# A convolution kernel before and after: the inverse transform over b in three tiles of 120 rows, one channel of its sums moved by DMA, and the stages issued as finer steps in another order

## The chip, the core and the metric

The kernel runs on one core of a Trainium2 chip. A core has five engines that run side by side and meet only at semaphores: TensorE (PE, matrix products; its weight loads are shown as PEld), VectorE (DVE), ScalarE (ACT), GpSimd (POOL) and SyncE (SP, which here only issues DMAs). Each works through its own instructions in order. The metric is the device time of one execution in microseconds.

## What is computed

The reference is a long convolution followed by two layers of experts, cut here to its lines of arithmetic:

```python
h_filt = (np.maximum(pos_emb @ w1, 0.0) @ w2) * np.exp(-0.01 * pos)[:, None]
u = x * v                                    # (2, 12480, 128)
y = np.fft.irfft(np.fft.rfft(u, n=2*S, axis=1) * np.fft.rfft(h_filt, n=2*S, axis=0)[None], n=2*S, axis=1)[:, :S, :]
x = (x * y).reshape(B * S, D)
h = x @ moe_w_in                             # 128 -> 2048
x = np.where(h > 0, h, np.exp(np.minimum(h, 0)) - 1) @ moe_w_out
h = x @ moe2_w_in
return (h * np.cos(h)) @ moe2_w_out
```

The kernel computes the convolution with a transform of its own. A sequence is laid out as NA = 98 rows (a) of NB = 128 (b), and the transform is taken over a (NF = 90 frequencies, real and imaginary part), twiddled, taken over b, multiplied by the transform of the filter, and taken back over b and then over a.

## The kernel before

The program has three stages. First the filter's taps are computed (to about 47 us). Then comes the convolution, to about 690 us: 32 chunks (NCH) of DC = 4 channels, each with three passes k: the two batches (k = 0, 1) and the filter (k = 2). The last stage runs the two expert layers (from about 694 us to the end). Beside the convolution the experts' weights are decoded in 32 jobs (`top` and `low`: small steps on ACT, DVE and GpSimd, and stores to `w_d`).

One pass of a chunk goes through these steps; the line numbers are those of the profile:

- `prod`: u = x * v on GpSimd (L321).
- `st_a`: four fp32 products over a into `ps_a` (L340, 180 columns each), two DVE products with the twiddles (za, zb, L345), one GpSimd sum (z, L348). For k = 2 ACT copies z to fp32r (zh, L97), and `lo_z` takes the rest (zl, L359) on GpSimd.
- `st_b`: the transform over b into `ps_b` (L376, 360 columns): four fp32 products for the batches, twelve fp32r products (high and low parts) for the filter. For the filter ACT copies the sums out (hr, hi, L381 to L383). For the batches DVE multiplies them by the filter's transform (L389, L390) and adds (y, L392); ACT copies y to fp32r (yh, L97), and `lo_y` takes the rest (yl, L332) on GpSimd.
- `st_c`: the inverse transform over b (L408). For each of the four channels the stationary operand is y's slice of 90 columns and the moving operand 256 columns of the table: six products for each channel, into its quarter of `ps_c` (90 partitions x 1024). Then two DVE products with the table ti (wa, wb, L412) and one GpSimd sum (w, L419; for the last chunk half of it on DVE, L417).
- `st_d`: the inverse transform over a (L426): two fp32 products of 512 columns, contracted over w's 90 partitions, into `ps_d`; DVE multiplies by x (at, L428), and SP stores it to `xt_d`, from where the experts' stage reads it.

An fp32 product is issued as two instructions in the trace. `ps_a`, `ps_b` and `ps_c` each have one pair of PSUM banks and `ps_d` one bank, so a product into such a buffer waits until the readers of its last contents are done. Where the last chunk's `ps_c` of k = 1 is concerned, it takes the pair of `ps_a`.

The order is written out by hand: within `tc.manual_schedule()` each engine issues in the order in which the program calls the steps. The tuple `steps` is the body of one period; an entry (f, back, k) runs step f for the chunk of `back` periods ago. So a chunk's passes are spread over three periods, and `st_c` and `st_d` of k = 1 run two periods after `st_a`. At the end of each period `load(p + 2)` issues the DMAs for x and v of a later chunk on SP. When the last period is through, ACT issues the loads of the first expert layer's weights and of its first x tile, which waits for the store of the last chunk's k = 0.

## Time and profile before

| | us |
|---|---|
| device time, median of 3 executions (lowest, highest) | 2923.79 (2923.07, 2927.09) |
| span of the profiled execution | 2922.3 |
| PE busy | 2888.7 (99%) |
| PEld busy | 2393.3 (82%) |
| DVE busy | 2497.0 (85%) |
| ACT busy | 2146.6 (73%) |
| POOL busy | 2632.8 (90%) |

The span counts from the first to the last instruction of the profiled execution; its own device time is not listed apart, and the median stands 1.5 us above the span. The busy shares are means over stages that differ: in the convolution ACT is busy for three tenths, among the experts for nearly nine. The granted TensorE clock, as a mean over the execution, is 0.995 of full speed; it is lower only at the start, at the run-in of the convolution (50 to 70 us) and between convolution and experts (690 to 710 us). A matmul's duration in the trace reaches into the next one, since they are pipelined; how long one takes of the engine's time is read from start to start.

### The profile page before, as it was taken

Reading aid. Unit: us, or ns where it says so; the run is one execution under the profiler, and the core shown is the slowest. Engines: PE = TensorE matmul, PEld = TensorE weight load, DVE = VectorE, ACT = ScalarE, POOL = GpSimd, SP = SyncE. Lnnn points to the kernel's source line nnn. Section 1 sums busy time; section 2 is a strip of 40 time slices with the busy share of each in tenths; the row PEclk is TensorE's granted clock in tenths of the full one; section 3 lists DMA queues with packets and bytes.
Section 4 is the critical chain, followed back from the end, with each engine's and each line's share of the span. In section 5 each row is a group of like instructions: output and inputs, shape, how many; then the busy total and the mean of one; then the engine's idle time right before and its main releaser. Section 6 shows DMA issues by size and latency. Waiting matters only on the chain.

```text
span 2922.3 us, 40341 instructions
## 1 busy us (share of the span) xinstructions
PE 2888.7 (99%) x13580; PEld 2393.3 (82%) x13580; DVE 2497.0 (85%) x3241; ACT 2146.6 (73%) x3332; POOL 2632.8 (90%) x1908
## 2 busy tenths in 40 slices
PE   8999999998999999999999999999999999999999
PEld 6878787886888888888888887888888888888887
DVE  5888888887998998899899998888888888888887
ACT  3322323224988898888888888888888888888887
POOL 4888888886999999999999998999999999999998
PEclk9999999998999999999999999999999999999999
DMA  3333333333000000000000001000000000000000
GB/s 105 90 81 88 97 89 86 88 83 97 14 11 14 11 12 14 14 11 11 14 11 14 11 11 60 11 14 11 14 11 14 11 11 14 11 14 11 13 12 14
DMA packets 83104, 96.82 MB, mean 33 GB/s; under 512 B 6106, under 2 KB 68088, under 8 KB 82898
## 3 DMA queue, kind: packets, MB, share of 16 engines
q1 hardware_dynamic: 77072, 88.20, 10.6%
q10 hardware_dynamic: 5826, 6.04, 0.7%
q8 instruction: 109, 1.79, 0.3%
q14 instruction: 97, 0.79, 0.1%
HBM read 59.94 MB, written 34.28 MB: 32 GB/s over the span
## 4 chain that ended last, share of the span: by engine, by line
PE 92%; ACT 3%; DVE 2%; issue 2%; POOL 1%; DMA 0%; ACTq 0%; POOLq 0%; DVEq 0%
PE h_ps L545 35%; PE o_ps L614 34%; PE ps_b L376 8%; PE ps_c L408 6%; PE ps_a L340 4%; PE ps_d L426 4%; ACT e L582 1%; DVE e L575 1%; DVE e L584 1%; ACT e L573 1%; PE h_ps L277 1%; ACT gh L97 1%; ACT ot L622 1%; PE w_ps L218 0%; PE r_ps L259 0%
## 5 line engine op out<-in xcount | busy, mean ns | idle before, releaser
L106 POOL TENSOR_TENSOR gl<-e,gh 128x960 fp32r<-128x960 f32 x780 | 1463.7, 1888 | 88.6 <-ACT gh L97 45.3
L545 PE MATMUL h_ps<-xh,w 128*128 128x480 f32 x3328 | 1022.3, 388 | 15.5 <-DVE e L562 5.5
L614 PE MATMUL o_ps<-gh,w 128*128 128x480 f32 x3120 | 933.0, 380 | 0.0
L545 PEld LDWEIGHTS h_ps<-xh,w 128*128 128x128 f32 x3328 | 623.0, 189 | 150.5 <-issue 26.6
L614 PEld LDWEIGHTS o_ps<-gh,w 128*128 128x128 f32 x3120 | 586.8, 188 | 92.9 <-POOL gh L105 0.2
L575 DVE SCALAR_TENSOR_TENSOR e<-e,h_ps 128x960 f32<-128x960 int32 x416 | 479.9, 1154 | 193.1 <-ACT e L573 67.0
L545 PE MATMUL h_ps<-xl,w 128*128 128x480 f32 x1664 | 634.6, 381 | 0.0
L560 DVE SCALAR_TENSOR_TENSOR e<-e,t_ps 128x480 f32<-128x480 f32 x832 | 539.6, 652 | 108.8 <-ACT t_ps L558 87.7
L614 PE MATMUL o_ps<-gl,w 128*128 128x480 f32 x1560 | 594.3, 381 | 2.0 <-POOL gl L106 2.0
L556 ACT ACTIVATE e<-h_ps 128x480 f32<-128x480 f32 x832 | 475.5, 572 | 141.6 <-PE h_ps L545 106.9
L573 ACT ACTIVATE e<-h_ps 128x960 int32<-128x960 f32 x416 | 404.1, 971 | 149.8 <-PE h_ps L545 148.0
L105 POOL TENSOR_SCALAR gh<-e 128x960 fp32r<-128x960 f32 x468 | 466.8, 998 | 42.1 <-DVE e L562 24.1
L558 ACT ACTIVATE t_ps<-h_ps 128x480 f32<-128x480 f32 x832 | 479.4, 576 | 0.0
L562 DVE SCALAR_TENSOR_TENSOR e<-e,h_ps 128x480 f32<-128x480 f32 x780 | 472.3, 647 | 0.0
L582 ACT ACTIVATE e<-e,half_pi 128x960 f32<-128x960 f32 x416 | 453.9, 1091 | 0.3 <-DVE e L575 0.3
L584 DVE TENSOR_TENSOR e<-e,h_ps 128x960 f32<-128x960 f32 x390 | 447.2, 1147 | 1.3 <-ACT e L582 1.2
L545 PEld LDWEIGHTS h_ps<-xl,w 128*128 128x128 f32 x1664 | 314.3, 189 | 52.3 <-POOL xl L106 0.6
L614 PEld LDWEIGHTS o_ps<-gl,w 128*128 128x128 f32 x1560 | 293.7, 188 | 50.6 <-POOL gl L106 3.2
L97 ACT ACTIVATE gh<-e 128x960 fp32r<-128x960 f32 x312 | 312.4, 1001 | 0.0
L376 PE MATMUL ps_b<-z_t,dft_t 128*128 128x360 f32 x512 | 165.7, 466 | 2.1 <-DVE y_t L392 1.7
L348 POOL TENSOR_TENSOR z_t<-za,zb 128x720 f32<-128x720 f32 x96 | 141.1, 1470 | 26.3 <-DVE zb L345 26.3
L408 PE MATMUL ps_c<-dft_h,yh 128*90 128x256 f32 x512 | 160.4, 313 | 0.0
(90 smaller groups left out, 3066.7 us busy)
## 6 DMA issues: line engine op xcount, KB each, us to landing
x_t<-in_x SPq DMA_DIRECT2D x32, 392.0 KB
v_t<-in_v SPq DMA_DIRECT2D x32, 392.0 KB
xt_d<-at SPq DMA_DIRECT2D x64, 196.0 KB
out<-ot SPq DMA_DIRECT2D x52, 240.0 KB
x_in<-xt_d SPq DMA_DIRECT2D x50, 240.0 KB
raw<-in_wi SPq DMA_DIRECT2D x16, 256.0 KB
w_d<-hi SPq DMA_DIRECT2D x32, 128.0 KB
w_d<-lo SPq DMA_DIRECT2D x32, 128.0 KB
```

The lines of the kernel that those rows point to most:

```text
L105: ENG[plan[0]].tensor_scalar(hi, full, 1.0, 0.0, op0=ALU.mult, op1=ALU.add)
L106: ENG[plan[1]].tensor_tensor(lo, full, hi.bitcast(F32), op=ALU.subtract)
L545: nc.tensor.matmul(h[:, 0:T], a, b, start=k == 0, stop=k == 2)
L556: nc.scalar.activation(u[:, e], hs[e][:, 0:T], AF.Exp)
L558: nc.scalar.activation(ts[e][:, 0:T], hs[e][:, 0:T], AF.Tanh, scale=0.5)
L560: nc.vector.scalar_tensor_tensor(u[:, e], u[:, e], 1.0, ts[e][:, 0:T], op0=ALU.add, op1=ALU.mult)
L562: nc.vector.scalar_tensor_tensor(gt[:, e], u[:, e], 0.0, hs[e][:, 0:T], op0=ALU.min, op1=ALU.max)
L573: nc.scalar.activation(kq, hv, AF.Copy, scale=1.0 / TWO_PI, bias=0.25)
L575: nc.vector.scalar_tensor_tensor(rr, kq, -TWO_PI, hv, op0=ALU.mult, op1=ALU.add)
L582: nc.scalar.activation(rr, rr, AF.Sin, bias=half_pi)
L584: nc.vector.tensor_tensor(gt, rr, hv, op=ALU.mult)
L614: nc.tensor.matmul(o, a, b[:, e], start=f == 0 and k == 0, stop=f == NFT - 1 and k == len(mm) - 1)
```

## The change

**Tiles of 120 rows.** y is written in another order: DVE's sum is split in two, so that the 4 x 90 columns of the four channels stand as three groups of 120: 90 columns of one of the first three channels and 30 of the fourth. The step `mm_c` takes each group as stationary operand: three tiles by six products, into 120 partitions x 768. The two products with ti and the sum w have that shape too. Rows 90 to 119 of w's three tiles are the fourth channel, in thirds; three DMAs on SP move them into a tile `v_w` of 90 partitions x 256. `mm_d` takes the first three channels from w (two products of 384 columns) and the fourth from `v_w` (two of 128). The table ti grows from 90 x 1024 to 120 x 1536 values.

**Filter products in another order.** In `mm_b` with k = 2 the eight products with zh come first and the four with zl last.

**Finer steps.** The stages are cut where they go from one engine to another: `mm_a` (A), `out_a` (a), `add_z` (z), `hi_z` (H), `lo_z` (L), `mm_b` (B), `out_h` (h), `mul_y` (y), `hi_y` (Y), `lo_y` (l), `mm_c` (C), `out_c` (c), `add_w` (w with its DMAs), `mm_d` (D), `out_d` (d), `prod` (u), `fetch` (x: the DMAs for x and v), `t` and `o` (the two halves of the decoding). One string gives the order: letter, periods back, pass. x and v are now fetched within the period, behind `d20`, for the chunk whose u is the period's last step. The last chunk's `ps_c` stays in its own pair of banks.

```diff
+NT = 3
+NM = DC * NF // NT
...
+    m = NM - NF
+    row = np.concatenate([np.repeat(np.arange(NF)[:, None], NT, 1),
+                          np.arange(m)[:, None] + m * np.arange(NT)[None, :]])[:, :, None]
+    ti = 2 * np.pi * ((2 * row + 1) * kr[None]) / (2 * L)
...
-            ti_t = const.tile([NF, 2, 4 * NB], F32, name="ti_t")
+            ti_t = const.tile([NM, 2, NT * 2 * NB], F32, name="ti_t")
...
+                def slot(n, name, at):
+                    return pa.tile([n, 2, 512], F32, name=name, tag=PS[at])
...
+                def mm_b(c, k, at):
...
+                        groups = (((dft_h, z[0]), (dft_l, z[0])), ((dft_h, z[1]),))
+                    for i, group in enumerate(groups):
+                        for r in range(2):
+                            mm = [(a[:, sl], b[:, q]) for sl, q in prs[r] for a, b in group]
+                            for j, (a, b) in enumerate(mm):
+                                nc.tensor.matmul(ps[:, r, 0:n], a, b, start=i == j == 0,
+                                                 stop=i == len(groups) - 1 and j == len(mm) - 1)
...
+                def mul_y(c, k, at):
...
-                    nc.vector.tensor_tensor(y, t1, pv[:, ::-1], op=ALU.add)
...
+                    q, m = pv[:, ::-1], NT * NF
+                    yv = y.rearrange("p r (i m) -> p r i m", i=NT)
+                    for o, a, b, e in ((slice(0, NF), 0, m, NT), (slice(NF, NM), m, n, NT)):
+                        nc.vector.tensor_tensor(yv[:, :, :, o], t1[:, :, a:b].rearrange("p r (i k) -> p r i k", i=e),
+                                                q[:, :, a:b].rearrange("p r (i k) -> p r i k", i=e), op=ALU.add)
+                    yy[c, k] = (y,)
+
+                def hi_y(c, k, at):
+                    yh = skewed(p2, [NB, 2, DC * NF], F32R, SKEW, name="yh")
+                    copy_r(yh, yy[c, k][0])
+                    yy[c, k] += (yh,)
...
+                def mm_c(c, k, at):
                     yh, yl = yy.pop((c, k))
-                    last = c == NCH - 1
-                    ps = pa.tile([NF, 2, 512], F32, name="ps_c", tag="ps_a" if last and k else "ps_c")
+                    ps = slot(NM, "ps_c", at or "c").rearrange("p a b -> p (a b)")
                     n = 2 * NB
-                    for s in range(DC):
-                        sl = slice(s * NF, (s + 1) * NF)
-                        o = ps[:, s // 2, (s % 2) * n:(s % 2 + 1) * n]
+                    for i in range(NT):
+                        sl = slice(i * NM, (i + 1) * NM)
                         mm = [(yt[:, r, sl], th[:, (1 - r) * NB:(3 - r) * NB])
                               for r in range(2) for yt, th in ((yh, dft_h), (yh, dft_l), (yl, dft_h))]
                         for j, (a, b) in enumerate(mm):
-                            nc.tensor.matmul(o, a, b, start=j == 0, stop=j == 5)
-                    t1 = p1.tile([NF, DC * n], F32, name="wa")
...
+                def out_c(c, k, at):
+                    ps, n = pcs.pop((c, k)), NT * 2 * NB
+                    t1 = p1.tile([NM, n], F32, name="wa")
+                    t2 = skewed(p1, [NM, n], F32, SKEW, name="wb")
                     for q, t in ((0, t1), (1, t2)):
-                        nc.vector.tensor_tensor(bank2(t), ps, ti_t[:, q:q + 1].to_broadcast([NF, 2, 512]), op=ALU.mult)
-                    w = p2.tile([NF, 2, DC, NB], F32, name="w_t")
-                    p, q = parts(t1, NB), parts(t2, NB)[:, ::-1]
-                    if last:
+                        nc.vector.tensor_tensor(t, ps[:, 0:n], ti_t[:, q], op=ALU.mult)
+                    wab[c, k] = t1, t2
+
+                def add_w(c, k, at):
+                    p, q = (t.rearrange("p (i r k) -> p i r k", i=NT, r=2) for t in wab.pop((c, k)))
+                    q = q[:, :, ::-1]
+                    w = p2.tile([NM, NT, 2, NB], F32, name="w_t")
+                    if c == NCH - 1:
                         nc.gpsimd.tensor_tensor(w[:, 0], p[:, 0], q[:, 0], op=ALU.add)
-                        nc.vector.tensor_tensor(w[:, 1], p[:, 1], q[:, 1], op=ALU.add)
+                        nc.vector.tensor_tensor(w[:, 1:NT], p[:, 1:NT], q[:, 1:NT], op=ALU.add)
                     else:
                         nc.gpsimd.tensor_tensor(w, p, q, op=ALU.add)
-                    ww[c, k] = w
-
-                def st_d(c, k):
-                    w = ww.pop((c, k))
-                    ps = pd.tile([NA, DC, NB], F32, name="ps_d")
-                    for r in range(2):
-                        nc.tensor.matmul(ps, g_t[:, r * NA:(r + 1) * NA], w[:, r], start=r == 0, stop=r == 1)
+                    v = p2.tile([NF, 2, NB], F32, name="v_w")
+                    m = NM - NF
+                    for i in range(NT):
+                        nc.sync.dma_start(v[i * m:(i + 1) * m], w[NF:NM, i])
+                    ww[c, k] = (w, v)
+
+                def mm_d(c, k, at):
+                    w, v = ww.pop((c, k))
+                    ps = pds[c, k] = pd.tile([NA, DC, NB], F32, name="ps_d")
+                    for o, rhs in ((ps[:, 0:NT], w[0:NF]), (ps[:, NT:DC], v.rearrange("p (i r) b -> p i r b", i=1))):
+                        for r in range(2):
+                            nc.tensor.matmul(o, g_t[:, r * NA:(r + 1) * NA], rhs[:, :, r], start=r == 0, stop=r == 1)
+
+                def out_d(c, k, at):
                     at = p2.tile([NA, DC, NB], F32, name="at")
-                    nc.vector.tensor_tensor(at, ps, xs[c][:, k], op=ALU.mult)
+                    nc.vector.tensor_tensor(at, pds.pop((c, k)), xs[c][:, k], op=ALU.mult)
...
-                steps = ((st_b, 1, 0), (prod, 0, 1), (top, 0, 0), (lo_y, 1, 0), (low, 0, 0), (top, 0, 1), (st_a, 0, 2),
-                         (st_c, 2, 1), (top, 0, 2), (lo_z, 0, 2), (low, 0, 1), (st_b, 1, 1), (st_a, 0, 0), (lo_y, 1, 1),
-                         (st_d, 2, 0), (low, 0, 2), (st_c, 1, 0), (prod, -1, 0), (st_b, 0, 2), (st_a, 0, 1), (top, 0, 3),
-                         (st_d, 2, 1))
-                for p in range(NCH + 2):
-                    for f, back, k in steps:
-                        if 0 <= p - back < NCH or f in (top, low):
-                            f(p - back, k)
-                    load(p + 2)
+                def fetch(c, k, at):
+                    if c not in xs:
+                        load(c)
+
+                FN = dict(u=prod, A=mm_a, a=out_a, z=add_z, H=hi_z, L=lo_z, B=mm_b, h=out_h, y=mul_y, Y=hi_y, l=lo_y,
+                          C=mm_c, c=out_c, w=add_w, D=mm_d, d=out_d, t=top, o=low, x=fetch)
+
+                def step(name, c, k, at=""):
+                    if name in "to" or 0 <= c < NCH:
+                        FN[name](c, k, at)
+
+                steps = """
+                    o t l10 a02 c21 B11 t y11 z02 H02 A00 D20 u01 C10 w21 a00 L02 d20 Y11 x-10 t
+                    z00 c10 B02 A01 a01 h02 l11 w10 z01 D21 o B00 t d21 y00 C11 A-12 Y00 o u-10
+""".split()
+                back = lambda s: (s[0], int(s[1:-1]) if len(s) > 1 else 0, int(s[-1]) if len(s) > 1 else 0)
+                for p in range(-2, NCH + 4):
+                    for f, b, k in map(back, steps):
+                        if f in "to" and not 0 <= p < NCH + 2:
+                            continue
+                        step(f, p - b, k)
```

How the order moves, at three places in the middle of the stage (names as in the code; the last figures are the shape that is written, "x4" stands for four alike). On TensorE, before, from A of k = 0 or 1 (`ps_a` from `u_t`) over D, B and the A of the filter (`ps_a` from `h_all`) to the first rows of a C tile:

```order
L340 MATMUL ps_a<-fa_t,u_t 128x180 x4
L426 MATMUL ps_d<-w_t,g_t 98x512 x2
L376 MATMUL ps_b<-z_t,dft_t 128x360 x4
L340 MATMUL ps_a<-fa_t,h_all 128x180 x4
L408 MATMUL ps_c<-dft_h,yh 90x256
L408 MATMUL ps_c<-dft_l,yh 90x256
```

The same place now:

```order
L342 MATMUL ps_a<-fa_t,u_t 128x180 x4
L463 MATMUL ps_d<-w_t,g_t 98x384 x2
L463 MATMUL ps_d<-v_w,g_t 98x128 x2
L385 MATMUL ps_b<-z_t,dft_t 128x360 x4
L432 MATMUL ps_c<-dft_h,yh 120x256
L432 MATMUL ps_c<-dft_l,yh 120x256
```

D is cut in two pairs, the second of which reads `v_w`; C comes ahead of the filter's A, which follows behind the tile, and writes 120 rows. On DVE, before, from D's `at` over the three y operations of k = 0 to the products with the filter's `ps_a` and with C's sums (`size` and `ps_w` are steps of the decoding):

```order
L428 TENSOR_TENSOR at<-ps_d,x_t 98x512
L389 TENSOR_TENSOR ya<-ps_b,hr 128x720
L390 TENSOR_TENSOR ps_b<-ps_b,hi_f 128x2x360
L392 TENSOR_TENSOR y_t<-ya,ps_b 128x720
L139 TENSOR_SCALAR size<-ps_w 128x256
L143 SCALAR_TENSOR_TENSOR ps_w<-ps_w,size 128x256
L345 TENSOR_TENSOR za<-ps_a,tw_t 128x720
L345 TENSOR_TENSOR zb<-ps_a,tw_t 128x720
L412 TENSOR_TENSOR wa<-ps_c,ti_t 90x1024
```

The same place now:

```order
L467 TENSOR_TENSOR at<-ps_d,x_t 98x512
L402 TENSOR_TENSOR ya<-ps_b,hr 128x720
L403 TENSOR_TENSOR ps_b<-ps_b,hi_f 128x2x360
L408 TENSOR_TENSOR y_t<-ya,ps_b 128x6x90
L408 TENSOR_TENSOR y_t<-ya,ps_b 128x6x30
L144 TENSOR_SCALAR size<-ps_w 128x256
L349 TENSOR_TENSOR za<-ps_a,tw_t 128x720
L349 TENSOR_TENSOR zb<-ps_a,tw_t 128x720
L440 TENSOR_TENSOR wa<-ps_c,ti_t 120x768
L440 TENSOR_TENSOR wb<-ps_c,ti_t 120x768
```

The sum y is written by two rows, and of the two decoding steps ahead of za and zb one has moved behind wb. On SP, before, one period's DMAs (`at`: stores of D's results, `raw`, `hi`, `lo`: the decoding's):

```order
L429 DMA xt_d<-at 98x4x128
L198 DMA x_t<-in_x 98x2x512
L199 DMA v_t<-in_v 98x2x512
L170 DMA w_d<-lo 128x256
L429 DMA xt_d<-at 98x4x128
L164 DMA w_d<-hi 128x256
L120 DMA raw<-in_wo 128x2x128
L429 DMA xt_d<-at 98x4x128
```

One period's now:

```order
L175 DMA w_d<-lo 128x256
L455 DMA v_w<-w_t 30x256 x3
L468 DMA xt_d<-at 98x4x128
L203 DMA x_t<-in_x 98x2x512
L204 DMA v_t<-in_v 98x2x512
L455 DMA v_w<-w_t 30x256 x3
L169 DMA w_d<-hi 128x256
L125 DMA raw<-in_wo 128x2x128
L468 DMA xt_d<-at 98x4x128
```

Two groups of three small DMAs have come in, one ahead of the store of k = 0 and of the loads of x and v, one behind these loads; the loads follow the store of k = 0 where they followed that of k = 1.

## Rows read from the trace of the kernel before

**Rows 1.** Busy time by stretches: start:end, length, then each engine, PEclk, DMA, GB/s.
```profile
160.26:649.00 488.74, 488.74 (x2699) 391.38 (x2698) 432.09 (x550) 145.81 (x300) 410.26 (x325) 1.00 0.33 89
649.00:2922.30 2273.30, 2249.69 (x10090) 1885.67 (x10088) 1945.00 (x2538) 1948.98 (x2928) 2111.61 (x1478) 1.00 0.05 17
```

**Rows 2.** Chain of waits, one period: start us, duration us, what, instructions.
```profile
201.29 2.83 PE ps_c L408 x24
204.12 2.42 PE ps_b L376 x8
206.54 1.22 PE ps_a L340 x8
207.76 1.72 PE ps_d L426 x4
209.48 2.82 PE ps_c L408 x24
212.30 1.99 PE ps_b L376 x12
214.29 1.22 PE ps_a L340 x8
215.51 1.72 PE ps_d L426 x4
217.23 2.42 PE ps_b L376 x8
219.66 1.22 PE ps_a L340 x8
```

**Rows 3.** Timeline of PE among the experts: start us, duration us, what.
```profile
713.27 0.60 PE L545 MATMUL h_ps<-xh,w 128*128 128x480 f32 x2
...
715.25 0.59 PE L614 MATMUL o_ps<-gh,w 128*128 128x480 f32 x2
```

**Rows 4.** Groups by shape, 160 to 649 us: busy us, mean ns, idle before.
```profile
L348 POOL TENSOR_TENSOR z_t<-za,zb 128x720 f32<-128x720 f32 x75 | 110.2, 1470 | 15.0 <-DVE zb L345 15.0
L419 POOL TENSOR_TENSOR w_t<-wa,wb 90x1024 f32<-90x1024 f32 x50 | 99.8, 1995 | 8.9 <-DVE wb L412 8.9
...
L345 DVE TENSOR_TENSOR za<-ps_a,tw_t 128x720 f32<-128x720 f32 x75 | 67.6, 901 | 16.2 <-PE ps_a L340 16.2
...
L408 PEld LDWEIGHTS ps_c<-dft_l,yh 128*90 128x90 f32 x400 | 62.8, 157 | 6.8 <-issue 6.8
...
L412 DVE TENSOR_TENSOR wb<-ps_c,ti_t 90x1024 f32<-90x1024 f32 x50 | 60.5, 1210 | 0.0
...
L97 ACT ACTIVATE yh<-y_t 128x720 fp32r<-128x720 f32 x50 | 40.0, 800 | 100.9 <-DVE y_t L392 100.9
...
L376 PEld LDWEIGHTS ps_b<-zh,dft_l 128*128 128x128 f32 x100 | 18.9, 189 | 0.0
```

**Rows 5.** Timeline of DVE, start of the y steps.
```profile
670.32 0.91 DVE L389 TENSOR_TENSOR ya<-ps_b,hr 128x720 f32<-128x720 f32 x1 [1.55 <-issue]
671.14 0.91 DVE L390 TENSOR_TENSOR ps_b<-ps_b,hi_f 128x720 f32<-128x720 f32 x1
```

**Rows 6.** Chain of waits at the end of the convolution.
```profile
667.81 2.42 PE ps_b L376 x8
670.23 2.84 PE ps_c L408 x24
...
673.13 2.66 PE ps_b L376 x8
...
688.67 2.36 DMA xt_d<-at
```

**Rows 7.** Timeline of SP: issue of a store.
```profile
310.62 0.33 SPq L429 DMA_DIRECT2D xt_d<-at  x1
```

**Rows 8.** Busy time by stretches: the stretch of one load of x and v.
```profile
316.50:322.50 6.00, 6.00 (x40) 5.29 (x39) 4.73 (x7) 1.62 (x3) 3.82 (x4) 1.00 0.74 185
```

**Rows 9.** Busy time by stretches: the end of the convolution.
```profile
680.00:690.00 10.00, 7.55 (x38) 4.56 (x37) 7.28 (x8) 0.00 (x0) 4.85 (x4) 1.00 0.88 281
```

More of the change, by code (lines that the diff above doesn't have):

```diff
@@ L315, in hyena_moe_kernel @@
                 bank = vs.enter_context(tc.tile_pool(name="bank", bufs=1, space=PSUM))
-                us, zz, yy, hh, ww = {}, {}, {}, {}, {}
-                def prod(c, k):
-                    if c < NCH:
-                        us[c, k] = p2.tile([NA, DC, NB], F32, name="u_t")
-                        nc.gpsimd.tensor_tensor(us[c, k], xs[c][:, k], vv[c][:, k], op=ALU.mult)
+                us, pas, za_, zz, pbs, hh, yy, pcs, wab, ww, pds = ({} for _ in range(11))
+                PS = {"a": "ps_a", "b": "ps_b", "c": "ps_c"}
                 def bank2(t):
@@ L346, in st_a, with add_z @@
                                                 tw_t[:, q:q + 1].to_broadcast([NB, 2, n]), op=ALU.mult)
+                    za_[c, k] = t1, t2
+                def add_z(c, k, at):
+                    t1, t2 = za_.pop((c, k))
                     z = p2.tile([NB, 2, DC * NF], F32, name="z_t")
@@ L367, in st_b @@
                     z = zz.pop((c, k))
-                    for r in range(2):
-                        for j, (sl, q) in enumerate(prs[r]):
-                            if k == 2:
-                                zh, zl = z
-                                mm = ((dft_h, zh), (dft_l, zh), (dft_h, zl))
-                            else:
-                                mm = ((dft_t, z),)
-                            for i, (a, b) in enumerate(mm):
-                                nc.tensor.matmul(ps[:, r, 0:n], a[:, sl], b[:, q], start=j == 0 and i == 0,
-                                                 stop=j == 1 and i == len(mm) - 1)
@@ L378, in st_b @@
-                    if k == 2:
-                        hr = p2.tile([NB, 1, n], F32, name="hr")
-                        hi = p2.tile([NB, 2, n], F32, name="hi_f")
-                        nc.scalar.activation(hr[:, 0], ps[:, 0, 0:n], AF.Copy)
-                        nc.scalar.activation(hi[:, 0], ps[:, 1, 0:n], AF.Copy)
-                        nc.scalar.activation(hi[:, 1], ps[:, 1, 0:n], AF.Copy, scale=-1.0)
-                        hh[c] = (hr, hi)
-                        return
+                    if len(z) == 1:
+                        groups = (((dft_t, z[0]),),)
+                    else:
+                        groups = (((dft_h, z[0]), (dft_l, z[0])), ((dft_h, z[1]),))
@@ new lines, in mm_b, with out_h @@
+                    for i, group in enumerate(groups):
[4 more added lines that the diff above has]
+                                                 stop=i == len(groups) - 1 and j == len(mm) - 1)
+                def out_h(c, k, at):
+                    ps, n = pbs.pop((c, k)), DC * NF
+                    hr = p2.tile([NB, 1, n], F32, name="hr")
+                    hi = p2.tile([NB, 2, n], F32, name="hi_f")
+                    nc.scalar.activation(hr[:, 0], ps[:, 0, 0:n], AF.Copy)
+                    nc.scalar.activation(hi[:, 0], ps[:, 1, 0:n], AF.Copy)
+                    nc.scalar.activation(hi[:, 1], ps[:, 1, 0:n], AF.Copy, scale=-1.0)
+                    hh[c] = (hr, hi)
```

58 lines of the change are left out of this document (28 added, 30 removed).

## The prediction, made before the change was run

> **What bounds the kernel now.** I read the trace by stretches first, then the chain of waits in one stretch, then the groups of instructions by shape. By stretches, the convolution stage (160 to 649 us) has TensorE busy for 488.74 of 488.74 us at the full granted clock, while DVE is busy for 432.09, GpSimd for 410.26 and ACT for 145.81; the DMA engines work a third of the time [rows 1]. The expert layers behind it, 2273 us, hold instructions that the change leaves alone [rows 1]. In the chain of waits one chunk of four channels is ten pieces of TensorE work, one behind the other without a gap: from 201.29 to 220.88, 19.59 us [rows 2]. 25 such periods fill the 488.74 us (24.95), and 32 make up the stage with its run-in and end. So here the sum of TensorE's work is the time, and the other three engines have 2.3, 3.1 and 13.7 us of each period free (488.74 less their busy time, over 25). What shortens TensorE's work shortens the stage, as long as no chain through the other engines becomes longer than the period.
>
> I call the pieces by the steps of the new code: A, B, C, D are TensorE's four products, a to d what DVE or ACT does with their sums, and the figure is the batch (0, 1) or the filter (2). A period is then C1, B1, A0, D0, C0, B2, A1, D1, B0, A2 in the order of [rows 2], counted from its first row.
>
> **C, the inverse transform over b.** Before: 4 channels by 6 products, 24 matmuls of 256 columns in 2.83 us, 0.118 us each, with 90 columns of weights. After: 3 tiles by 6, 18 matmuls of the same 256 columns, with 120 columns of weights. No row has 120, but three shapes of the same number type stand on both sides: 0.118 us for 256 columns (90 of weights), 1.99/12 = 0.166 for 360 (128 of weights) [rows 2], and nine matmuls between 713.27 and 715.25, 0.220 for 480 (128 of weights) [rows 3]. Per moving column these are 0.461, 0.461 and 0.458 ns: the spacing follows the moving columns and not the weights. I take 0.118 us: 18 x 0.118 = 2.12 us, **0.71 us less per tile**, 1.42 per period. The bound against it: weight loads take 157 ns with 90 columns and 189 with 128 [rows 4], so some 26 ns more with 120; were all of that to show, a tile would take 18 x 0.144 = 2.59 us and save 0.24. Downwards the bound is 0.118.
>
> The Trainium skill ("TensorE: Matmul & The Clock Gate", LDWEIGHTS) says that a weight load lasts columns/1.2 ns, so 25 ns more for 120 than for 90; the loads' rows grow by 0.84 ns per column and agree. Its section on the back-to-back gap also lets both operations set the spacing of load and matmul pairs, which would be the bound of 2.59 us; against that stands that 128 columns of weights cost nothing per moving column in the rows.
>
> **D.** Two products of 512 columns become two of 384 and two of 128, each as two instructions. From 1.72/4 = 0.430 us for 512 columns and 1.22/8 = 0.1525 for 180 [rows 2] one column costs 0.836 ns, so 0.323 and 0.109: 4 x 0.432 = 1.73 us, 0.01 more. Below 180 columns no row exists; if a short one were held by its weight load (157 to 189 ns), D would take up to 0.3 more. I take 0.01.
>
> **Other TensorE work.** A, B0 and B1 are as before; B2's twelve products are the same in another order, the low parts last. On TensorE only A2 and C1 change places. The new period is 19.59 - 2 x 0.71 + 2 x 0.01 = **18.19 us**, laid out from B1: B1 0 to 2.42, A0 3.64, D0 5.37, C0 7.49, B2 9.48, A1 10.70, D1 12.43, B0 14.85, C1 16.97, A2 18.19.
>
> **Do the others keep up?** DVE: each of the four products of c falls from 1024 to 768 elements. 1210 ns against 901 for 720 [rows 4] is 1.02 ns an element, so 950 ns: 1.04 us less per period. Each y sum becomes two adds (540 and 180 elements, still 720): one more fixed part. By the same slope a 720-element operation has 0.17 us that don't shrink, of which 0.08 overlap with the next one (0.82 from start to start of the first two in [rows 5]), so 0.09 us; the bound above is that the short add comes wholly on top, 0.17 + 180 x 0.00102 = 0.35. DVE then needs 17.28 - 1.04 + 0.18 = 16.4 of 18.19 us. GpSimd: w goes from 1.995 us to 1.55 (1.470 for 720 elements [rows 4]), twice: 16.41 - 0.89 = 15.5. Both fit, with less than two and three microseconds over. So it is the order that decides, and I follow the four tightest chains.
>
> *B0, y, B1* (one bank pair for B). In the end stretch of before nothing stands between: B0 ends at 670.23, B1 starts at 673.13, so the y steps with all hand-overs take 2.90 us [rows 6]. With the split 2.99 (bound 3.25). TensorE now has C1 and A2 in between, 3.34 us. Slack 0.35, at worst 0.09.
> *A2, a2, A0* (one pair for A). Two operations of 720 elements, 0.82 + 0.90 [rows 4, 5], and hand-overs of 0.2: 1.92 of the 2.42 that B1 takes. Slack 0.5.
> *y1 before B2.* On DVE a2 ends at 1.8, c1 (two of 0.87) at 3.55, a decode step at 3.9, y1 at 6.65; B2 starts at 7.49. Slack 0.7.
> *C1, c, w, DMA, D1.* c1 at 3.55. GpSimd has yl (its input is ready when y0, at 17.7, and ACT's 0.80 us copy [rows 4] are done: 0.3 in the next period), z, u, each at most z's 1.47, and then w: 0.3 + 3 x 1.47 + 1.55 = 6.3. SP then issues three DMAs; a store's issue takes 0.33 [rows 7], so the third starts at 7.1. A store of before landed 2.36 us after its issue began [rows 6]: 9.4. D1's second pair, the first to read it, is due at 10.70 + 4 x 0.323 = 12.0. Slack 2.6. For batch 0 the same transfer has most of a period.
>
> What is queued: SP is in order, and the next store and the x and v loads stand behind the w wait. They are issued after d0, about 9. The burst of such a load lasts some 6 us at 0.74 of the DMA engines [rows 8], so it lands at about 15.5; u of the next chunk is GpSimd's last step and is needed by A0 at 18.19 + 2.42 = 20.6. With 1.5 us for u itself, hidden with 3.6 us over; without that cover it would cost what it is late.
>
> **The end of the stage.** There C1 now waits for c0 (the other bank pair is no longer used for the last chunk), D0 waits for the moved channel, and the store that the experts' first load needs is issued behind three more DMAs. Before, that store is issued 20.86 us after the last B0 starts (667.81 to 688.67) [rows 6]. Laid out the same way after the change: B0, C1, B1 until 8.0, D0 9.8, C0 11.9, c0 13.7, C1 15.9, c1 17.7, w share 18.3, three issues, store at 19.3. Three C tiles less would have given 18.7, so **0.5 us lost**. While this runs, the weights of the first expert layer fill the DMA engines to 0.88 [rows 9]; if the moved channel queues behind them, up to 4 us. I take 0.5. The run-in has TensorE's steps in the same order, so I put it at nothing. The larger table (0.72 instead of 0.36 MB) is loaded before the stage and first read in c; at the burst's 185 GB/s [rows 8] it holds other loads up by 2 us at most, and I take none of it.
>
> **Sum.** 64 tiles x (0.708 - 0.01) = 44.7, less 0.5: 44.2 us. The profiled execution has a span of 2922.3 us, 1.5 below the median of 2923.79; the same difference goes off both. 2923.8 - 44.2 = **2879.6**, rounded 2880.
>
> **Rivals.**
> *A chain through DVE sets the period.* For: slacks of 0.35 and 0.5 us where before 1.15 and more stood (A2 and C1 between B0 and B1, 4.05 us). Against: even the bound of 3.25 fits. If each of the two adds cost as much as the whole one did, the y steps would take 2.90 + 0.82 = 3.72, 0.38 over: 0.38 x 32 = 12 us lost, more if hand-overs add to it: 2892 to 2898.
> *Weight loads show.* 0.24 instead of 0.71 per tile: 15 us gained, 2909. The Trainium skill's rule above is this case; the three equal costs per column speak against it.
> *D1 waits for the moved channel, and the kernel gets slower.* Its place is D1's second pair in every period. If the three small DMAs land behind a load burst instead of ahead of it, they come at 7.1 + 6 + 2.4 = 15.5 instead of 9.4, 3.5 us late: 3.5 - 1.4 = 2.1 us more per period, 67 over 32 periods, 2991. It decides from a landing 6.3 us after the third issue (at 12.0 + 1.4). For: SP is in order, and the transfers share the engines with 1.7 MB per period (89 GB/s [rows 1]). Against: in SP's new order the loads come behind these three, and the previous burst ends at about 15.5 of the period before, 9 us ahead of them.
>
> **How the numbers follow.** TensorE bound throughout: 0.70, at 2874 to 2886. DVE chain: 0.14, 2888 to 2900. Weight loads: 0.05, about 2909. D1 late by just the gain: 0.03, about 2924. Slower: 0.08, up to 2991. The range 2874 to 2900 holds the first two, 0.84, and with it the half-hidden middle values; its lower end is C at 0.118 with 5 us from a shorter run-in. A measurement here tells about 0.2% (6 us) from no change. Faster 0.89, same 0.03, slower 0.08.
>
> **What would show it.** Right: a period of 18.2 us in the chain of waits, all of it TensorE; C tiles of 18 matmuls in 2.12 us; 128-column matmuls in D at about 0.11 us. Wrong: spacing in C of 0.14 us (weight loads); idle time of TensorE before B1 put down to DVE's y, or before D's second pair put down to the DMA; DVE waiting nowhere. A gap of some microseconds longer at 650 to 690 would be the end of the stage.

## The result and the profile after

The changed kernel takes 2882.18 us (median of 2879.27 to 2882.80) where the kernel before takes 2924.68 us (2923.07 to 2927.09): a ratio of 0.9854, 95% interval 0.9841 to 0.9867, 42.5 us less. The forecast was 2880 in a range of 2874 to 2900, with 0.89 on faster. The profiled execution of after, 2879.27 us, is the lowest of its four (span 2877.5), so the sums below are checked against medians too.

By stretches, as [rows 1]: start:end, length, busy us of PE, PEld, DVE, ACT, POOL, then PEclk, DMA share, GB/s.

```profile
155.00:610.00 455.00, 454.80 (x2598) 376.75 (x2598) 406.39 (x600) 145.95 (x300) 388.90 (x324) 1.00 0.38 107
670.00:2877.00 2207.00, 2194.18 (x9833) 1844.39 (x9831) 1899.40 (x2474) 1927.34 (x2888) 2074.14 (x1449) 1.00 0.05 14
```

The convolution is still TensorE's alone. Its chain of waits for one period (start us, duration us, what, instructions), the counterpart of [rows 2]:

```profile
301.25 2.42 PE ps_b L385 x8
303.67 1.22 PE ps_a L342 x8
304.89 1.73 PE ps_d L463 x8
306.62 2.12 PE ps_c L432 x18
308.74 1.97 PE ps_b L385 x12
310.72 1.22 PE ps_a L342 x8
311.94 1.73 PE ps_d L463 x8
313.67 2.42 PE ps_b L385 x8
316.09 2.12 PE ps_c L432 x18
318.21 1.22 PE ps_a L342 x8
```

Ten pieces without a gap from 301.25 to 319.43: 18.18 us where the forecast had 18.19 and [rows 2] 19.59. Both C tiles lost 0.71 us, D got 0.01 dearer. From the first B0 of chunk 0 to that of chunk 31 the kernel before needs 603.4 us (64.20 to 667.64), the changed one 561.5 (62.01 to 623.51): 42 us less over 61 of the 64 tiles.

The groups by shape in the stage, for [rows 4] (busy us, mean ns):

```profile
L451 POOL TENSOR_TENSOR w_t<-wa,wb 120x768 f32<-120x768 f32 x50 | 77.3, 1546 | 0.0
L432 PEld LDWEIGHTS ps_c<-dft_l,yh 128*120 128x120 f32 x300 | 54.5, 182 | 3.0
...
L440 DVE TENSOR_TENSOR wb<-ps_c,ti_t 120x768 f32<-120x768 f32 x50 | 47.4, 949 | 0.0
```

The c products are 949 ns (950 forecast), w 1546 (1550). A weight load did grow from 157 to 182 ns, as feared in the bound, but the 18 matmuls still follow one another at 0.118 us.

Two places were not as forecast. The first is SP, whose issues are shown here over half a period (start us, us spent, line, what, count):

```profile
307.27 3.50 SPq L455 DMA_DIRECT2D v_w<-w_t  x3
310.88 0.50 SPq L468 DMA_DIRECT2D xt_d<-at  x1
311.42 0.87 SPq L203 DMA_DIRECT2D x_t<-in_x  x1
```

Three small transfers hold SP for 2.5 to 3.5 us, not for the 1.0 us that a store's 0.33 [rows 7] let expect, and the store and the loads stand behind them. In the waits of the stretch from 155 to 610 (us in total, times, longest), u then stands 15.4 us for v, but TensorE only once, for 0.2 us, for the moved channel:

```profile
POOL u_t L335 <- DMA v_t<-in_v: 15.4, 23, 1.5
...
PE ps_d L463 <- DMA v_w<-w_t: 0.2, 1, 0.2
```

The second is the end of the stage, in the chain of waits (for [rows 6]):

```profile
634.56 3.64 DMA v_w<-w_t
...
640.55 3.22 DMA v_w<-w_t
...
645.23 0.78 SPq L455
646.06 0.78 SPq L455
...
646.94 2.52 DMA xt_d<-at
```

On this chain D waits for the moved channel twice, and the last store stands behind its last issues. From the start of the last B0 (623.51) to that store (646.94) it is 23.4 us, against 21.0 before (667.64 to 688.67; the 20.86 of [rows 6] count from 667.81, where the chain has the end of the piece ahead) and 19.3 laid out. This store is the last chunk's of batch 0, the one that the experts' first load waits for; it is called the last store below, though batch 1's follows some 3 us later.

### The profile page after: what moved, and what is told of

Its sections match the earlier page's. It is cut to its first block, busy times and chain, and to the rows that moved or that the text cites. A ratio compares the mean times of both kernels' runs of the same rounds, so it can differ in the third digit from the quotient of the medians.

```text
span 2877.5 us, 40599 instructions
## 1 busy us (share of the span) xinstructions
PE 2842.1 (99%) x13452; PEld 2371.8 (82%) x13452; DVE 2465.6 (86%) x3305; ACT 2145.1 (75%) x3332; POOL 2604.1 (90%) x1908
## 4 chain that ended last, share of the span: by engine, by line
PE 91%; DVE 3%; ACT 3%; issue 2%; POOL 1%; DMA 1%; SPq 0%; POOLq 0%; ACTq 0%; DVEq 0%
PE h_ps L595 36%; PE o_ps L664 35%; PE ps_b L385 7%; PE ps_c L432 4%; PE ps_a L342 4%; PE ps_d L463 3%; DVE e L625 1%; ACT e L632 1%; DVE e L634 1%; ACT e L623 1%; PE h_ps L282 1%; ACT gh L102 0%; PE w_ps L223 0%; ACT ot L672 0%; DMA v_w<-w_t 0%
## 5 line engine op out<-in xcount | busy, mean ns | idle before, releaser
L625 DVE SCALAR_TENSOR_TENSOR e<-e,h_ps 128x960 f32<-128x960 int32 x416 | 480.1, 1154 | 192.0 <-ACT e L623 67.8
L102 ACT ACTIVATE yh<-y_t 128x720 fp32r<-128x720 f32 x64 | 51.6, 806 | 208.4 <-DVE y_t L408 208.4
```

The costliest lines, as they stand in the source:

```text
L625: nc.vector.scalar_tensor_tensor(rr, kq, -TWO_PI, hv, op0=ALU.mult, op1=ALU.add)
```

## The experiments

Differences are in medians against the changed kernel's 2882.2 us unless a kernel is named. "Stage" is the time from the first B0 of chunk 0 to that of chunk 31, "end" from the latter to the issue of the last store, both from the profiled execution, and so each from one execution.

**1 and 2. The order without the tiles, and the tiles without the order.** The theory was that six matmuls fewer per tile are the gain; the rival, that the finer order is.

```
 e1: after, but   mm_c: for s in range(DC): 6 matmuls, weights yt[:, r, 90 columns]
                  mul_y: one add; add_w: no dma_start; mm_d: two matmuls of 512
 e2: before, with the three tiles, the split add and the dma_starts
                  in its own st_b, st_c and st_d; its steps and their order stay
```

> The finer steps in the new order, but the inverse transform over b in four tiles of 90 rows as before: 24 matmuls per tile, one y add, four products of 1024 elements, two matmuls of 512 columns in D, nothing moved by DMA. Theory 1 (the gain is six matmuls fewer per tile on TensorE, and the order alone is worth only what it does to the run-in): the period stays 19.6 us, the first B0 starts at 62.0 instead of 64.2, B0 of chunk 0 to B0 of chunk 31 takes 603 us as before; the end of the stage loses up to 2 us, since C1 of the last chunk waits for the products of c0. Time 2920 to 2926. Rival (the order takes out waits, and a good part of the gain is its own): a period under 19.3 us and at most 2910.

> The three tiles of 120 rows, the split y add and the moved channel put into the kernel before, whose coarse steps and their order stay. Theory 1: the period is 18.2 us (TensorE is the bound and six matmuls fewer per tile are the whole of it), run-in as before (first B0 at 64.2), B0 of chunk 0 to B0 of chunk 31 561 to 563 us, end of the stage 3 to 5 us longer than 20.9; time 2881 to 2887. Rival (the tiles need the new order: in the old one the products of c, the sums and the DMA stand right behind one another in front of other steps, and TensorE waits for DVE or for the moved channel): TensorE shows gaps before B1 or D's second pair, the period is 18.6 us or more, and the time 2893 or more.

Measured: order alone 2925.4 us, ratio 1.0005 (0.9995 to 1.0014) to before; tiles alone 2886.0, ratio 0.9868 (0.9853 to 0.9883). Stage 605.2 and 562.3 us. In the chain of waits of the first kernel C is 24 matmuls again, and the period (from one A2 to the next, 300.54 to 320.13) 19.59:

```profile
307.12 2.83 PE ps_c L429 x24
```

and in the stretch of the second TensorE has no idle time at all, in the coarse order of before:

```profile
155.00:610.00 455.00, 455.00 (x2603) 377.98 (x2602) 409.22 (x601) 146.25 (x301) 387.97 (x327) 1.00 0.39 107
```

So the tiles are the gain, and the rival falls. The order is worth some 3.8 us on top of the tiles: by the profiles 2.8 in the run-in (from the first A2 to the first B0 13.8 us with the tiles alone, 11.0 with both), 1.1 at the end (24.6 and 23.4) and 0.8 in the stage. Without the tiles it is worth nothing that can be measured: the first B0 comes 2.0 us sooner than before (62.2), but the stage is 1.8 us longer and the end 1.1 (22.1), with C1 waiting for c0.

A part of these differences is TensorE's clock. Ahead of the first B1 TensorE waits 1.7 to 1.8 us in both kernels, the changed one and that with the order alone:

```profile
67.65 2.66 PE L385 MATMUL ps_b<-z_t,dft_t 128*128 128x360 f32 x8 [1.76 <-POOL full L163]
```
```profile
67.76 4.35 PE L385 MATMUL ps_b<-z_t,dft_t 128*128 128x360 f32 x8 [1.70 <-DVE y_t L405]
```

In the first the granted clock stays at 1.00; in the second it falls to 0.50 (the 1.2 GHz level) from 67.8 to 71.2, and B1 takes 1.7 us more. The profiles of experiments 1, 2, 5 and 10 have such a fall of 3.4 us near 70 us, and in each the first period is 1.6 to 1.7 us longer (16.6 to 16.7 instead of 15.0, in experiment 1 17.3 instead of the 15.7 before). That is nearly all of the 1.8 us of the order alone. With the tiles alone it is more than the 0.8: there the stage without its first period is 0.8 us shorter than in the changed kernel.

**3, 4 and 8. The end of the stage.** The theory was that the moved channel is on the path there; the rival, that the experts' weight loads hold the end anyway.

```
 e3: after, but if c == NCH - 1: four tiles of 90 rows, no dma_start
 e4: after, but without the three dma_starts; D reads one tile of zeros
 e8: e3, and also (c, k) == (NCH - 2, 1); C1 of the last chunk in tag "ps_a"
```

> The changed kernel, but the last chunk of four channels goes by four tiles of 90 rows, with nothing moved by DMA. Theory 1 (at the end of the stage the moved channel is on the path: its three issues of about 0.86 us on SP ahead of the last stores, and its landing 3.2 to 3.6 us after the issue while the experts' weights are loaded): TensorE does 1.4 us more in the two tiles of the last chunk, D of that chunk waits no longer for a DMA, and the last store of the stage is issued 2 to 3 us sooner after the last B0 (20.5 to 21.5 us instead of 23.4). Time 2 to 3 us less than the changed kernel's. Rival (the experts' weight loads hold the end anyhow): from the last B0 to the last store 23 us or more, and the time no less.

> The changed kernel without the three DMAs per tile: D's second pair reads a tile of zeros that is set once, so the last channel of each four is wrong from there on. Theory 1 (the DMA is hidden in the steady state and costs only at the end): period 18.2 us and 561.5 us from B0 of chunk 0 to B0 of chunk 31, as with the DMAs; SP's next loads of x and v are issued some 3 us sooner, and u no longer waits for v (15 us in 23 waits before); from the last B0 to the last store some 4 us less (19.3 instead of 23.4). Time 3 to 5 us less than the changed kernel's. Rival (the moved channel stands at the edge in every period and costs there too): a period of 18.1 us or less, at least 3 us less from B0 of chunk 0 to that of chunk 31, and 7 us or more in all.

> The changed kernel, but the last chunk and batch 1 of the one before it go by four tiles of 90 rows without DMA, and C1 of the last chunk takes the idle bank pair of A, as before the change. Theory 1 (of the 22.1 us from the last B0 to the last store with the last chunk alone undone, the wait of D1 of the chunk before for the moved channel, 1.4 us, and the wait of C1 for the products of c0, about 1 us, go too): 19.5 to 20.5 us, time 2877 to 2880, 3 to 5 us less than the changed kernel's. Rival (the weight loads of the experts hold the stores whatever the tiles): 21.5 us or more and a time as with the last chunk alone undone, 2880.

Measured: end 22.1, 19.8 and 21.1 us (23.4 in the changed kernel); times 2879.8, 2877.3 and 2881.7. Without any transfer DVE goes from c1 over its share of w to the product d as laid out, and the last store follows at 642.70 with no issue ahead of it:

```profile
640.39 0.95 DVE L443 TENSOR_TENSOR wb<-ps_c,ti_t 120x768 f32<-120x768 f32 x1
641.37 0.69 DVE L452 TENSOR_TENSOR w_t<-wa,wb 120x512 f32<-120x512 f32 x1
641.98 0.68 DVE L467 TENSOR_TENSOR at<-ps_d,x_t 98x512 f32<-98x512 f32 x1
```

The end is 19.8 us, against 19.3 laid out with three issues of 0.33 us: so the moved channel costs 3.6 of the 23.4. In the stage it costs next to nothing: 560.7 us without it and 561.5 with it. This settles theory against rival. One expectation missed: u still waits for v, 13.9 us in 23 times, so it is not the small transfers' issues that hold the loads back (they stand behind the store, which waits for d0). As versions to use, the two repairs bring less: their ends are 1.3 and 2.4 us shorter, each 0.6 us longer than the upper end that I expected, and in the medians 2.4 and 0.5 us show (of the second 3 to 5 were expected), within the spread of the runs (2876 to 2883 for both). Neither can be called faster than the changed kernel.

**5 and 6. Who issues the moved channel, and where on SP.** The theory was that only the place in SP's order matters, and that it matters much.

```
 e5: w10 ... v10 Y00   and   Y11 v21 x-10    (step v: the three DMAs, nc.scalar)
 e6: w10 v10           and   x-10 v21        (step v: the three DMAs, nc.sync)
```

> The changed kernel with the three DMAs of the moved channel issued by ACT instead of SP, as a step of their own: batch 1 right behind the ACT copy of y1, batch 0 right ahead of the copy of y0. Theory 1 (SP's 2.5 to 3.5 us per tile for these issues only delay what stands behind them, and in the steady state nobody on the path waits for that): period 18.2 us, 561 to 562 us from B0 of chunk 0 to B0 of chunk 31; the waits of u for v (15 us) are gone; at the end of the stage the stores no longer stand behind three issues, but the issues now stand in ACT's queue beside the experts' weight loads: last B0 to last store 21 to 23 us instead of 23.4; time 0 to 2 us less than the changed kernel's. Rival (ACT becomes late: 3 us of issues ahead of the copy of y0 delay yh, then yl, then C): gaps of TensorE before C, a period of 18.4 us or more, time 2888 or more.

> The changed kernel with one step moved on SP: batch 1's three DMAs of the moved channel are issued behind the next loads of x and v instead of ahead of them. This is the place of the forecast's rival on the slower side. If the small transfers wait behind the loads (rival as it was priced: landing 3.5 us late or more per period), TensorE waits before D1's second pair in every period: with issues of 0.85 us, store at 310.9, loads until 313.2, the third small issue at about 315 on the clock of the changed kernel's period, where D1's second pair stood at 313.1; if they land 2.3 us after it, 4 us late per period, 125 us in 31 periods, about 3005; if they land only with the burst, 6 us later, 8 us late, about 3130. The other theory (the order on SP is of no weight, since the transfers overtake the loads and the loads then start sooner): less than 1 us per period, at most 2910.

Measured: from ACT 2895.7 us, 13.5 more; behind the loads 3082.0 us, 200 more, ratio 1.0545 to before. The theory missed on the first, whose time is the rival's (2888 or more), though TensorE has no gap before C, where the rival put it; on the second it held. The Trainium skill ("DMA: Bandwidth & Descriptors", Rules for kernel authors) says that spreading transfers over several issuing engines gives no bandwidth and saves issue time only; here the saved time of SP was paid by ACT. On ACT the end itself was as expected (22.7 us), but the stage became 567.2 us, and the issues stood in ACT's queue ahead of the experts' weights and of x_in:

```profile
641.01 13.87 ACTq L459 DMA_DIRECT2D v_w<-w_t  x9
654.92 4.20 ACTq L562 DMA_DIRECT2D w<-w_d  x8
659.63 0.59 ACTq L577 DMA_DIRECT2D x_in<-xt_d  x1
```

x_in is asked for at 659.6, 7.2 us after the store's issue (2.6 in the changed kernel), and the first expert product starts 14.4 us after that issue instead of 6.2: 5.7 in the stage, 8.2 here and 0.7 won at the end give 13.2 of the 13.5. In the stage the list of waits shows D waiting 3.5 us for the moved channel, four times, and 3.8 us of idle time in all between 155 and 610; of the rest of its 5.7 us, 1.7 lie in the first period, with the clock at 0.50 from 68.2 to 71.6.

Behind the loads, D1 waits in every period, in the same list from 155 to 610:

```profile
PE ps_d L467 <- DMA v_w<-w_t: 77.9, 18, 5.4
```

4.3 us each on average. The stage is 192 us longer, 6.2 per period: the wait, and more that follows it, since DVE, ACT and GpSimd wait behind TensorE (in the same list ACT's yh stands 248 us for y, 12.3 the longest; 162 and 4.5 in the changed kernel), and the granted clock of this stretch is 0.90 instead of 1.00. The rival on the slower side is therefore real. What keeps it away is the order on SP.

**11. How near is it?** One or three more DMAs of 30 rows ahead of the three.

```
+                    for i in range(1):          # e11_three_more: range(3)
+                        nc.sync.dma_start(v2[i * m:(i + 1) * m], w[NF:NM, i])
```

> The changed kernel with one more DMA of 30 rows per tile on SP ahead of the three of the moved channel, into a tile that nobody reads: 0.8 us later. Theory 1 (in the steady state the third issue starts at about 310.0, lands 2.1 us later, at 312.1, and D1's second pair reads it at 313.1: a margin of 1.0 us, not the 2.6 of the forecast): hidden or nearly, D1 waits in a few periods for 0.2 us at most; B0 of chunk 0 to B0 of chunk 31 561.5 to 563 us, time 0 to 4 us more. Rival (no margin is left): 0.8 us in every period, 25 us more.

> The same with three more: 2.5 us later. Theory 1 (margin of 1.0 us): D1's second pair waits about 1.5 us for the moved channel in every period, 1.5 to 1.8 us x 31 = 45 to 55 us more, 2927 to 2940, no faster than the kernel before. Rival (the margin of 2.6 us that the forecast gave): hidden, at most 5 us more.

Measured: 2885.1 (2.9 more) and 2936.5 us (54.3 more; 1.0048 to before, 1.0033 to 1.0063: slower). With one more, TensorE waits three times in 25 periods; with three, in nearly each:

```profile
PE ps_d L466 <- DMA v_w<-w_t: 0.8, 3, 0.4
```
```profile
PE ps_d L466 <- DMA v_w<-w_t: 27.2, 22, 2.2
```

One period of the latter, in its chain of waits:

```profile
412.25 0.65 PE ps_d L466 x4
...
428.94 0.78 SPq L458
429.77 2.04 DMA v_w<-w_t
...
431.94 0.65 PE ps_d L466 x4
```

19.69 us instead of 18.18: 2.5 us of issues, 1.5 of them to be seen, a net margin of 1.0 us as the theory had it; 2.5 us more on SP turn the change into a loss. The way to it is another one, though. In the changed kernel the third issue starts 7.8 us after B1 (309.01) and not at 310.0, and with a landing 2.0 us later nearly 2 us are free. But the loads of x and v stand behind the issues: u's waits for v grow from 15.4 to 87.5 us between 155 and 610, GpSimd's w ends later (by 0.6 us in the median of the periods), and the issues start later by that once more.

**7. The y chain.** One or three more DVE sums of 180 elements in batch 0's y step.

```
+                    for _ in range(1 if k == 0 else 0):      # e7_y_plus3: 3
+                        nc.vector.tensor_tensor(y[:, :, 0:90], t1[:, :, 0:90], pv[:, :, 0:90], op=ALU.add)
```

> The changed kernel with one more DVE operation in the y step of batch 0, a sum of 180 elements that the next ones overwrite: 0.25 us from start to start (the two adds take 0.97 us together, the longer one 0.72). Theory 1 (slack of 0.35 to 0.5 us between the end of the y step and the start of B1): hidden, the same period of 18.2 us and the same time within 2 us. Rival (DVE sets the period already): 0.25 x 32 = 8 us more, about 2890.

> The same with three more of these sums in the y step of batch 0: 0.75 us. Theory 1 (slack of 0.35 to 0.5 us): 0.25 to 0.4 us past it in every period, TensorE waits before B1 for DVE's y, period 18.45 to 18.6 us, 8 to 13 us more: 2890 to 2895. Rival (the chain has room, DVE is idle for 2 us of each period): the same time within 2 us. Rival (DVE sets the period): 0.75 x 32 = 24 us more, 2906.

Measured: 2890.7 (8.5 more) and 2916.0 us (33.8 more). That is the rival's number in the first, and more than every theory in the second. The cause is two sizes that I had wrong, and the slack is one of them. DVE with one more sum, TensorE's A2 and B1 there, and A2 and B1 at the same place of the changed kernel:

```profile
413.14 0.34 DVE L406 TENSOR_TENSOR y_t<-ya,ps_b 128x180 f32<-128x180 f32 x1
413.51 0.97 DVE L410 TENSOR_TENSOR y_t<-ya,ps_b 128x540 f32<-128x540 f32 x2
```
```profile
413.25 1.38 PE L342 MATMUL ps_a<-fa_t,h_all 98*128 98x180 f32 x8
414.63 2.66 PE L385 MATMUL ps_b<-z_t,dft_t 128*128 128x360 f32 x8
```
```profile
427.16 1.38 PE L342 MATMUL ps_a<-fa_t,h_all 98*128 98x180 f32 x8
428.38 2.58 PE L385 MATMUL ps_b<-z_t,dft_t 128*128 128x360 f32 x8
```

The extra sum takes 0.37 us from start to start, not 0.25. The last add ends at 414.48 and B1 starts at 414.63, 1.38 us after A2's start; in the changed kernel it is 1.22. So B1 is 0.16 us late, though the trace shows no gap: the end that it gives to A2's last matmul (428.55 in the changed kernel) lies 0.16 us behind the point at which the next matmul starts when nothing holds it up (428.38). The eight matmuls themselves then take 0.07 us more, all of it in the first. That makes a period of 18.43 us (408.69 to 427.12), 0.24 more, and the busy column has no idle time for it: TensorE is busy for 454.92 of 455 us there. With three more sums, 1.13 us, B1 starts 0.93 us late and takes the same 0.07 more: 1.00, against 33.8/31 = 1.09 measured (the first period alone has 4.0 more, with the clock at 0.50 from 68.1 to 74.9); the waits show 18.5 us in 24 times, 0.77 each:

```profile
PE ps_b L385 <- DVE y_t L410: 18.5, 24, 1.1
```

Both leave the same slack, 0.37 - 0.24 and 1.13 - 1.00: 0.13 us, not 0.35. In the changed kernel itself the last add of that step ends 2.83 us after B0, with a hand-over of 0.16 that is 2.99, so the forecast's chain of y stands. What it has to keep up with was too long: C1 and A2 fill 3.34 us to the end that the chain gives A2, but B1 starts 0.16 us ahead of that end, and its first weight load another 0.15 ahead (428.23). DVE's 2 us of free time per period were of no help.

**10. The run-in.** B2's products back in the old order.

```
-                        groups = (((dft_h, z[0]), (dft_l, z[0])), ((dft_h, z[1]),))
+                        groups = (((dft_h, z[0]), (dft_l, z[0]), (dft_h, z[1])),)
```

> The changed kernel with the twelve products of B2 in the order of before: high, low and the low part of z in turn, so that the third product already needs zl. Theory 1 (the run-in's gain of 2.2 us comes from this: in the run-in TensorE waited 0.5 us for zl and its clock came back 3 us later): first B0 at 63.5 to 64.2 instead of 62.0; period 18.2 us as before; time 1.5 to 2.2 us more than the changed kernel's. Rival (the gain comes from the decode step that DVE no longer does ahead of a02): first B0 at 62.0 to 62.5 and the time within 0.5 us.

Measured: 2885.5 us, 3.3 more (1.5 to 2.2 expected). The first B0 is at 63.05, below the 63.5 expected; but the run-in starts at different moments in different executions (the first A2 at 49.6 to 51.7 in those looked at). From the first A2 to the first B0 it is 13.4 us, 11.0 in the changed kernel and 13.2 in that before, so the rival falls: DVE's order is the new one here. The two ways of B2 in TensorE's timeline, the changed kernel and the old order:

```profile
57.68 0.73 PE L385 MATMUL ps_b<-zh,dft_h 128*128 128x360 f32 x1
...
59.35 0.33 PE L385 MATMUL ps_b<-zh,dft_l 128*128 128x360 f32 x1
...
62.01 2.66 PE L385 MATMUL ps_b<-z_t,dft_t 128*128 128x360 f32 x8
```
```profile
57.72 0.67 PE L385 MATMUL ps_b<-zl,dft_h 128*128 128x360 f32 x1 [0.57 <-POOL zl L368]
...
60.58 0.50 PE L385 MATMUL ps_b<-zl,dft_h 128*128 128x360 f32 x1
...
63.05 2.59 PE L385 MATMUL ps_b<-z_t,dft_t 128*128 128x360 f32 x8
```

The third product waits for zl in the old order, and all twelve take 0.50 us or more; in the new order nothing waits, and from the sixth on (59.35) they take 0.33. The granted clock is 0.50 (the 1.2 GHz level) until 59 and 1.00 from 60 in the changed kernel, and with the old products 0.50 until 62 and 1.00 from 63. So the gain of the run-in is B2's order: TensorE works on without a gap, and in these two executions the clock is back three microseconds sooner. Its size scatters: in the profiles of all eleven kernels with the new order the run-in takes 10.7 to 12.0 us, in the three with the old one (before, experiments 2 and 10) 13.2 to 13.8, so that 11.0 is near the lower end and 1.7 us lie between the middle values. The stage (563.4 us) and the end (24.6) were also longer here, by 1.9 and 1.2 us. Of the former 1.7 lie in the first period, with the clock at 0.50 from 69.6 to 73.1; the latter I can't explain.

## Why the prediction was right, point by point

**The bound and C's term held, and they are the result.** A period of 18.18 us for 18.19, C at 0.118 us per matmul. The run with the last chunk undone has both widths of weights within seven microseconds of TensorE's timeline:

```profile
626.41 0.28 PE L479 MATMUL ps_c<-dft_h,yh 128*120 128x256 f32 x1
626.53 0.28 PE L479 MATMUL ps_c<-dft_l,yh 128*120 128x256 f32 x1
...
633.11 0.28 PE L440 MATMUL ps_c<-dft_l,yh 128*90 128x256 f32 x1
633.22 0.28 PE L440 MATMUL ps_c<-dft_h,yl 128*90 128x256 f32 x1
```

0.12 us from start to start with 120 columns and with 90. The rival in which the weight loads show is out. The Trainium skill ("TensorE: Matmul & The Clock Gate", LDWEIGHTS) makes a load's time grow with its columns, and the loads did (157 to 182 ns, 0.83 ns per column); what its section on the back-to-back gap would make of that, a spacing set by loads and matmuls together, these rows don't show.

**D and the other engines** came as worked out: 1.73 us per D; DVE 406.39/25 = 16.3 us of a period (16.4 forecast), GpSimd 15.6 (15.5). The rival with DVE's chain did not come, but by less than was forecast: by 0.13 us and not 0.35 (experiment 7). Its price was put too low with that: two adds at the cost of a whole one each, 0.73 us more than measured, would have been 0.6 over and not 0.38, some 19 us and not 12 (an estimate from these two figures, over 32 periods).

**The moved channel: right outcome, one term mis-sized.** "A store's issue takes 0.33" was carried over to the small transfers; they take 0.8 each, as the loads of x and v did before the change (0.84 and 0.82). The w sum ends at 307.24, 6.0 us after B1's start (6.3 forecast), but the third issue starts at 7.8 (309.01) instead of 7.1. A landing 2.0 us later, as in experiment 11, gives 9.8 against a need at 11.8 (313.07): 2.0 of slack instead of 2.6. Not every period has it: in three, at 531, 550 and 568 us, the transfer landed only 4.1 to 4.2 us after the third issue began, D was late, and the periods took 18.40 to 18.55 us. These three make up the 0.8 us by which the stage is longer than without the transfers; why they landed late stays open. u, too, has less: it ends at 319.17 and A0 starts at 321.85, 2.7 us over instead of 3.6.

**The slower rival** had the right mechanism and place, and the right reason against it: SP's order. Its price, 3.5 us late per period, was too low: when the loads do go first, D waits 4.3 us, and the period is 6.2 us longer.

**The end of the stage: the step that failed.** "I take 0.5" where the bound, 4 us, came true: 18.9 us without any loss (21.0 less three times 0.71), 23.4 measured, 4.5 lost. Experiment 4 puts 3.6 of that on the moved channel and leaves 0.9; in experiment 1, where nothing is moved and C1 waits for c0, the end is 1.1 longer than before. The 3.6 are landings of 3.2 and 3.6 us while the weights fill the DMA engines, and issues of 0.8 us ahead of the last store.

**The run-in: put at nothing, 2.2 us in fact.** "TensorE's steps in the same order" overlooked the order of the products inside B2, which the prediction itself names under the other TensorE work.

**The sum.** Stage 41.9 less and run-in 2.2 less, end 2.4 more, and 0.4 more from the last store to the first expert product, make 41.3 us, and in the profiled executions the first expert product comes 41.3 us sooner (694.41 to 653.09). The medians differ by 42.5. Of the forecast's 44.2 the profiles miss 2.9: 4.0 at the end, 0.7 in the stage (42.6 for its 61 tiles) and 0.4 behind it, against 2.2 won in the run-in. The two failed terms have opposite signs and cancel in part, so the sum looks better than its parts.

What lies behind the first expert product, which the change does not touch, took 2224 to 2231 us in the profiled executions of these fourteen kernels whatever the convolution was. In this stretch the granted clock stood at 0.50 for 5.3 us (2224.0 us) to 19.4 us (2231.2 us); less half of that time, it is 2219.5 to 2221.8 us in all fourteen, so most of the scatter goes with the clock. Differences of 3 us between kernels are to be read from the stage, not from the total, and in the stage from the periods behind the first.

## What to carry to other kernels

Where one engine's chain is the time, a sum over its instructions at measured cost per column is a good forecast; spend the remaining effort on the hand-overs, for a transfer that is new has to be costed with a row of its own kind (source, rows per transfer), not with the nearest store. A slack that is counted to the end which the trace gives a matmul is too large, since the next one starts ahead of that end, and the busy column does not show the loss: read start-to-start times. An edit that is free in the steady state is to be costed again at both ends of the stage, where queues are shared with other work.

## What was not expected of the hardware

- Issuing one transfer of 30 rows (30 KB) from SBUF to SBUF took SP 0.78 to 0.86 us, in single cases up to 1.76, against 0.33 to 0.60 for a store of 196 KB; it landed 2.0 us after its issue began in a quiet period, 3.2 to 3.6 us while the experts' weights were loaded, and in three periods of the stage 4.1 to 4.2.
- A group of matmuls that had to wait 0.16 us shows no idle time ahead of it, and its first matmul took 0.07 us more: 0.24 us per period, all of it counted as busy.
- Behind the same wait of 1.7 to 1.8 us ahead of the first B1 the granted clock fell to 0.50 in some executions and stayed at 1.00 in others; a fall of 3.4 us there cost 1.6 to 1.7 us.
- Weight loads grew from 157 to 182 ns without any change in the spacing of 0.118 us.
